# A Fourier mixing and SwiGLU kernel: earlier projection halves, an earlier rows load and later conversions in the head of the first batch

## Chip, cores and metric

The kernel runs on one core of a Trainium2 chip. The metric is the device time of one execution in microseconds (us); the time of a version is the median of several executions.

## The reference

Two blocks follow each other. The first mixes the 3008 positions of a sequence with a Fourier filter, for 8 sequences of 256 channels. The second is a SwiGLU network over the 8 x 3008 = 24064 rows that result.

```python
X = np.fft.rfft(x, axis=1)                       # x: (8, 3008, 256)
Y = X * (filt_r + 1j * filt_i)[None, :, :]       # filters: (1505, 256)
y = np.fft.irfft(Y, n=3008, axis=1)
g = y @ w_gate                                   # (24064, 256) @ (256, 1536)
silu = g * (1.0 / (1.0 + np.exp(-g)))
out = (silu * (y @ w_val)) @ w_out               # (1536, 256)
```

The three weight matrices arrive as 64-bit floats. The kernel itself has to turn them into 32-bit floats, from their bits.

## The kernel before

**Spectral part.** The transform of length 3008 = 47 x 64 is made of small dense transforms, each a matrix product on TensorE. For the first batch (`Spectral(0)`), stage 1 (`stage1_first`, then `turn`) transforms over 47 rows; stage 2a (L886) multiplies by a table, and VectorE (DVE) multiplies the result by the filter (L895, L899, L904), GpSimd (POOL) adds the two halves (L328); stage 2b (L921) multiplies by the table of the way back. There are 12 pieces u of stage 2 (`N_TWO`), and stage 2b runs four pieces behind stage 2a. ScalarE (ACT) copies each piece out of PSUM (L929) into a tile g. Each piece must then be regrouped before stage 3 (`stage3`, L970), which gives the tokens' values: pieces below `N_STORED` are stored to a tensor d2 in DRAM (`store_rest`) and read back into f0 by one load (`load_rows`), issued from POOL's queue; the later pieces go from g to f0 by small row copies on SP's queue (L934). Stores of the later pieces to d2 follow, since the chunks k = 1 to 3 of the batch are read from there (`load_t4`, L670, tile t). TensorE runs products on zeros (`idle`, L591) where it has nothing else to do.

**Network part.** The work is cut into chunks k of the sequence and groups g of hidden units (`Group`). One pair (k, g) is a step; a batch has 12. `SCHEDULE` is a list of 174 tokens that sets by hand the order of all instructions of a step on every engine; TensorE's hidden products are L1064, the output products L1161. Token t0.0 is the first product of the next chunk's stage 3 (tile pd). `combine_sequence` makes the sums of token values that some products need. Only in batch 0 are the steps ordered by g outside and k inside.

**Preparation of the weights.** `weight_halves` lists 36 halves of weights: for each of three groups 8 hidden halves ("hid") and 4 projection halves ("proj"). `load_weights(i)` loads half i (256 KB). `round_half(i)` rounds it, one step per call: DVE masks the mantissa (L405) and shifts the exponent (L408); ScalarE converts the mantissa (L410); the exponent is clamped either by DVE (L414, L417) or by ScalarE (L421, L423, L425); DVE puts in the sign (L428) and adds the low word (L432); POOL multiplies mantissa and exponent (L440, or L452 and L453) and makes sums. `combine_weights` makes further sums of hidden weights. The class `Preparation` gives each such step a tick: half i has a base tick, 4 after that of the half before (16 after half 7), and its steps follow at fixed distances. Ticks are executed at places written by hand: some between the pieces of stages 1 and 2, then at the places `tick_at` of each step of batch 0; `finish` executes what is due. So a tick is no time: it places instructions in the engines' program order. Buffers are few: raw words, `pw` (three) and w (two, and one in `wo_t` for every third half) are used again by later halves. `pin` fixes the order as written.

The order around the change: after stage 2a of piece 11, POOL loads halves 8 to 11 (L1255), then the rows; `finish(0)` runs the ticks up to 44; stage 2b of pieces 8 to 11 follows; SP issues the row copies, the stores of pieces 8 to 11 and the loads for chunk 1.

Of the kernel before, what the change touches and what calls it, by code (L numbers as in the profile page):

```python
# [43 lines left out]
AF = mybir.ActivationFunctionType  # L44
# [12 lines left out]
NK = 4 * NS  # L57
# [12 lines left out]
NV = 2  # L70
N_ONE = 32 // NV
N_TWO = NS // NV
N_QUAD = 8
N_FOUR = NS // 4
N_STORED = 8


WO = {1: 0, 7: 1, 2: 2, 3: 3, 5: 4, 6: 5, 4: 6}
# [25 lines left out]
BLOCKS = (0, 1, 3, 2)  # L104
# [101 lines left out]
def kernel(  # L206
# [10 lines left out]
    nc = tc.nc  # L217
# [157 lines left out]
        return spot if i < N_LENT and spot < 3 else None  # L375

    N_EARLY = 12

    def load_weights(i, queue=nc.sync):
        if i in raws or i >= len(weights):  # L380
# [9 lines left out]
    def round_half(i):  # L390


        raw, (use, *at) = raws[i], weights[i][1]
        low, high = raw[:, :, :, 0], raw[:, :, :, 1]
        pw = rpool.tile([128, 2, 128], U32, name=f"pw_{i}", tag="pw", bufs=3)
        if i % 3 == 2 and i < N_LENT:
            w = wo_t.rearrange("p j i f -> p (j i f)")[:, NJ * 7 * 128 - 256:]
            w = w.rearrange("p (b f) -> p b f", b=2)
        else:
            w = rpool.tile([128, 2, 128], FP32, name=f"w_{i}", tag="w", bufs=2)  # L400
        man = w.bitcast(U32)
        v = nc.vector
        flat = "p b f -> p (b f)"
        flat2 = "p b f two -> p (b f) two"
        pin(v.tensor_scalar(out=man, in0=high, scalar1=0xFFFFF, scalar2=None,  # L405
                            op0=ALU.bitwise_and))
        yield
        pin(v.tensor_scalar(out=pw, in0=high, scalar1=20, scalar2=0x7FF,  # L408
                            op0=ALU.logical_shift_right, op1=ALU.bitwise_and))
        pin(nc.scalar.activation(out=w, in_=man, func=AF.Copy, scale=2.0 ** -20, bias=1.0))  # L410
        yield
        pf = pw.bitcast(FP32)
        if i < 2 * len(BLOCKS):
            pin(v.tensor_scalar(out=pf, in0=pw, scalar1=-896.0, scalar2=0.0,  # L414
                                op0=ALU.add, op1=ALU.max))
            yield
            pin(v.tensor_scalar(out=pw, in0=pf, scalar1=255.0, scalar2=2.0 ** 23,  # L417
                                op0=ALU.min, op1=ALU.mult))
            yield
        else:  # L420
            pin(nc.scalar.activation(out=pf, in_=pw, func=AF.Relu, bias=off_t))  # L421
            yield
            pin(nc.scalar.activation(out=pf, in_=pf, func=AF.Relu, bias=top_t, scale=-1.0))  # L423
            yield
            pin(nc.scalar.activation(out=pw, in_=pf, func=AF.Copy, scale=-(2.0 ** 23),  # L425
                                     bias=255 * 2.0 ** 23))
            yield
        pin(v.scalar_tensor_tensor(out=pw.rearrange(flat), in0=raw.rearrange(flat2)[:, :, 1],  # L428
                                   scalar=0x80000000, in1=pw.rearrange(flat),
                                   op0=ALU.bitwise_and, op1=ALU.bitwise_or))  # L430
        yield
        pin(v.scalar_tensor_tensor(out=w.rearrange(flat), in0=raw.rearrange(flat2)[:, :, 0],  # L432
                                   scalar=2.0 ** -52, in1=w.rearrange(flat),
                                   op0=ALU.mult, op1=ALU.add))
        yield
        e = nc.gpsimd
        if use == "proj":
            j, l = at
            dst = wo_t[:, j]
            pin(e.tensor_tensor(out=dst[:, ts(l, 2), :], in0=w, in1=pf, op=ALU.mult))  # L440
            yield
            if l:
                b11, b12, b21, b22, t1, t2, t4 = [dst[:, i] for i in range(7)]
                pin(sub(e, t1, b12, b11))
                pin(sub(e, t2, b22, t1))
                pin(sub(e, b12, b22, b12))
                pin(sub(e, t4, b21, t2))
            return
        g, i, z = at
        wt = weights_of(0, 0, g)  # L450
        x, y, u = w[:, 0], wt[:, SLOT[f"Q{i}"], z], wt[:, SLOT[f"P{i}"], z]
        pin(e.tensor_tensor(out=y, in0=w[:, 1], in1=pf[:, 1], op=ALU.mult))  # L452
        pin(e.tensor_tensor(out=x if KS[i] else u, in0=x, in1=pf[:, 0], op=ALU.mult))  # L453
        yield
        if KS[i] == -1:
            pin(sub(e, u, x, y))
        elif KS[i]:
            pin(add(e, u, x, y))
            if KS[i] == 2:
                pin(add(e, u, u, y))  # L460
# [28 lines left out]
    class Preparation:  # L489
# [3 lines left out]
        def __init__(self):  # L493
            self.at, self.held = 0, []

            self.ticks, self.need = {}, {}
            base, ready = [], {}

            def put(t, f, by, pool=False):
                self.ticks.setdefault(t, ([], []))[pool].append(f)  # L500
                self.need[by] = max(self.need.get(by, 0), t)

            for i, (_, (use, *at)) in enumerate(weights):
                hid, g = use == "hid", at[0] if use == "hid" else at[0] // JB
                by = ((0, 3, 6) if hid else (1, 4, 7))[g]
                b = base[-1] + (4 if i != 2 * len(BLOCKS) else 16) if i else 0
                if i >= N_EARLY:
                    same = [n for n in range(N_EARLY, i) if spot_of(n) == spot_of(i)]
                    k = 2 if spot_of(i) is None else 1
                    last = base[same[-k]] + 8 if same[k - 1:] else 0  # L510
                    b = max(b, last + 8)
                    put(max(last, b - 10), lambda i=i: load_weights(i), by)
                base.append(b)
                if hid and g == NG - 1:
                    ready.setdefault(NT, b)
                half = []

                def go(half=half, i=i):
                    if not half:
                        half.append(round_half(i))  # L520
                    next(half[0], None)

                times = (0, 1, 2, 3, 4, 6, 7, 9, 10) if i >= 2 * len(BLOCKS) else \
                    (0, 1, 2, 3, 4, 6, 9, 10)
                for t in times:
                    put(b + t, go, by, t > 8 or t == 7)
                if hid and at[1:] == [BLOCKS[-1], 1]:
                    for n, pair in enumerate(PAIRS_USED):
                        c = combine_weights(g, *pair)
                        for t in range(3):  # L530

                            put(b + 11 + n + t, lambda c=c: next(c, None),
                                by if g or n < 4 else 1, t == 2)
            self.barriers = sorted((t, step) for step, t in ready.items())
            self.end = max(self.ticks)
# [22 lines left out]
        def finish(self, step):  # L558
            while any(s <= step and self.at <= t for s, t in self.need.items()):
# [1 line left out]
                self.tick(step)  # L561

    preparation = Preparation()
    tick_at = [set(range(40, 162, 6)), *[{n * 174 // 20 for n in range(20)}] * 2,
               {0, 6, 12, 18, 24, 31, 37, 42, 72, 78, 84, 90, 96, 102, 108, 114, 122, 130, 138, 146}]

    back_t, quad_t = [], []
# [26 lines left out]
    class Spectral:  # L594
# [345 lines left out]
            rows = self.d2_tokens.rearrange("n (p s) c -> (n p) (s c)", p=2)  # L940
            pin(queue.dma_start(out=rows[:, ts(u, NV * C)], in_=g.rearrange("q s c -> q (s c)")))

        def store_rest(self):

            for u, g in self.rest:
                self.load(out=self.d2_parts[:, ts(u, NV)], in_=g)
            self.rest = []

        def stage3(self, k, step):
# [241 lines left out]
    with tc.tile_pool(name="start", bufs=1) as spool0:  # L1191
# [12 lines left out]
        n = 0  # L1204
# [36 lines left out]
        for u in range(N_TWO + lag):  # L1241
            if u < N_TWO:
                spec.turn(u + 2)
                step = spec.stage2a(u)
                next(step)
                if u % 3 == 1:
                    spec.real_part(u + 2)
                next(step)
                preparation.tick(0, 2 * (u < 3), hold=True)
                run(step)  # L1250
                preparation.release()
                if u % 3 != 2:
                    spec.real_part(u + 1)
            if u == N_TWO:
                for i in range(8, N_EARLY):  # L1255
                    load_weights(i, nc.gpsimd)
                spec.load_rows(f0[0:8 * N_STORED, 0:2 * NH], 0, slice(0, 2 * N_STORED),
                               slice(0, 2 * NH), nc.gpsimd)
            if u == N_TWO + lag - 1:
                preparation.finish(0)  # L1260
            if u >= lag:
                if u == N_TWO:
                    idle(zero, [bank("idle")], 512)
                run(spec.stage2b(u - lag))
            if u == 6:
                pin(nc.sync.dma_start(out=wi_t, in_=wi_dram.ap()))
        for i in range(2):
            spec.t4[0, i] = f0[0:NK, ts(i, NH), :]
        spec.store_rest()
        for i in range(2):  # L1270
            spec.load_t4(1, i)

        idle(zero, [bank("idle") for _ in range(5)], 512)
        for step in (0, 2, 1, 3):
# [222 lines left out]
```

## Time and profile before

| | |
|---|---|
| median of 3 executions | 2826.43 us (2824.17 to 2828.59) |
| profiled execution | 2824.58 us |
| its span, first to last instruction | 2822.8 us |
| mean granted TensorE clock | 0.996 of full |
| TensorE busy | 2785.6 us (99%) |
| VectorE, ScalarE, GpSimd busy | 1994.4, 1565.0, 1573.9 us |
| data moved by DMA | 586.61 MB, mean 208 GB/s |

The profile comes from one execution, whose time is the span and what lies around it. PE is TensorE's matmuls, PEld its weight loads, SP the engine that only issues DMAs; SPq, ACTq and POOLq are issues of DMAs. In a timeline a row gives start and duration in us, engine, line, operation, the tile written and the tile read, and in brackets how long the engine stood idle before, and what ended that. A view of stages gives for each stretch the busy us of each engine with the number of instructions, the granted clock, the share of time that the DMA engines were busy and the GB/s moved. A matmul of 32-bit floats appears as two passes. Instructions of one engine run in program order, so one that waits holds up all behind it.

The first batch's spectral head takes the first 79 us; step 0 runs from there to about 108 us; steps 1 and later take about 29 us each.

### The profile page before, as it was taken

Reading aid. Unit: us, or ns where it says so; the run is one execution under the profiler, and the core shown is the slowest. Engines: PE = TensorE matmul, PEld = TensorE weight load, DVE = VectorE, ACT = ScalarE, POOL = GpSimd, SP = SyncE. Lnnn points to the kernel's source line nnn. Section 1 sums busy time; section 2 is a strip of 40 time slices with the busy share of each in tenths; the row PEclk is TensorE's granted clock in tenths of the full one; section 3 lists DMA queues with packets and bytes.
Section 4 is the critical chain, followed back from the end, with each engine's and each line's share of the span. In section 5 each row is a group of like instructions: output and inputs, shape, how many; then the busy total and the mean of one; then the engine's idle time right before and its main releaser. Section 6 shows DMA issues by size and latency. Waiting matters only on the chain.

```text
span 2822.8 us, 48516 instructions
## 1 busy us (share of the span) xinstructions
PE 2785.6 (99%) x15442; PEld 2319.7 (82%) x15442; DVE 1994.4 (71%) x4575; ACT 1565.0 (55%) x4182; POOL 1573.9 (56%) x1680
## 2 busy tenths in 40 slices
PE   8999999999999999999999999999999999999998
PEld 6777888888888888788888888878888888888886
DVE  7788776767666766667766677667676767666666
ACT  5776455655555555555555555555554555555553
POOL 4786575465545565456653566445655455545544
PEclk9999999999999999999999999999999999999999
DMA  8687876877666775667666676667766777654543
GB/s 224 201 276 244 272 243 212 288 234 238 181 188 203 248 224 172 204 216 229 221 184 198 210 250 198 189 189 239 225 207 178 215 224 229 190 155 145 153 136 82
DMA packets 363206, 586.61 MB, mean 208 GB/s; under 512 B 198348, under 2 KB 246476, under 8 KB 362792
## 3 DMA queue, kind: packets, MB, share of 16 engines
q1 hardware_dynamic: 338406, 534.17, 60.8%
q10 hardware_dynamic: 22354, 44.41, 5.8%
q0 software_dynamic: 2192, 4.91, 0.7%
q8 instruction: 126, 2.06, 0.3%
q14 instruction: 128, 1.05, 0.1%
HBM read 467.61 MB, written 101.34 MB: 202 GB/s over the span
## 4 chain that ended last, share of the span: by engine, by line
PE 91%; DVE 2%; POOL 1%; DMA 1%; ACT 0%; issue 0%; SPq 0%; POOLq 0%; ACTq 0%; DVEq 0%
PE wa L1064 25%; PE wk L1064 17%; PE wA L1161 17%; PE we L1064 12%; PE wG L1161 8%; PE wF L1161 4%; PE pd L967 3%; PE wqa L705 2%; PE wqc L764 1%; PE wqb L776 1%; DMA lent<-later_tbl 0%; PE pa L846 0%; POOL out_dram L1146 0%; POOL h L331 0%; PE pb L886 0%
## 5 line engine op out<-in xcount | busy, mean ns | idle before, releaser
L1064 PE MATMUL wa<-y_t,wt_t 128*128 128x188 f32 x4464 | 878.5, 323 | 3.9 <-ACT m L1099 2.7
L1064 PEld LDWEIGHTS wa<-y_t,wt_t 128*128 128x128 f32 x4464 | 746.8, 190 | 80.0 <-ACT wa L1090 8.9
L1064 PEld LDWEIGHTS wk<-y,wt_t 128*128 128x128 f32 x2976 | 495.4, 190 | 106.9 <-issue 33.4
L1064 PE MATMUL wk<-y,wt_t 128*128 128x188 f32 x2976 | 572.6, 325 | 0.8 <-ACT f L1079 0.8
L328 POOL TENSOR_TENSOR h<-h 128x376 f32<-128x376 f32 x190 | 183.5, 987 | 696.9 <-DVE h L1111 690.7
L331 POOL TENSOR_TENSOR h<-h 128x376 f32<-128x376 f32 x572 | 557.8, 997 | 15.4 <-DVE h L328 15.2
L1161 PE MATMUL wA<-h,wo_t 128*128 128x376 f32 x1532 | 550.9, 482 | 2.8 <-DVE o L328 2.1
L1064 PE MATMUL we<-y_t,wt_t 128*128 128x188 f32 x2232 | 431.8, 323 | 1.1 <-ACT we L1095 0.9
L331 POOL TENSOR_TENSOR D<-f,f 128x376 f32<-128x376 f32 x288 | 280.3, 987 | 257.3 <-ACT f L1079 253.6
L331 DVE TENSOR_TENSOR we<-we,m 128x376 f32<-128x376 f32 x576 | 319.9, 556 | 139.2 <-PE we L1064 71.3
L1064 PEld LDWEIGHTS we<-y_t,wt_t 128*128 128x128 f32 x2232 | 369.3, 190 | 2.3 <-ACT we L1095 1.7
L1161 PEld LDWEIGHTS wA<-h,wo_t 128*128 128x128 f32 x1532 | 275.3, 190 | 111.2 <-issue 7.2
L1099 ACT COPY m<-wa 128x376 f32<-128x376 f32 x576 | 272.6, 473 | 100.2 <-PE wa L1064 97.3
L335 DVE SCALAR_TENSOR_TENSOR y<-wk,c 128x376 f32<-128x376 f32 x480 | 244.5, 540 | 62.1 <-ACT c L1083 37.9
L1106 ACT ACTIVATE g<-wa 128x188 f32<-128x188 f32 x576 | 187.4, 326 | 165.3 <-PE wa L1064 155.9
L1106 ACT ACTIVATE u<-we 128x188 f32<-128x188 f32 x576 | 188.6, 327 | 160.4 <-DVE we L331 152.4
L1161 PE MATMUL wG<-h,wo_t 128*128 128x376 f32 x768 | 274.1, 479 | 0.0
L1083 ACT COPY c<-wk 128x376 f32<-128x376 f32 x288 | 136.5, 474 | 223.8 <-PE wk L1064 199.0
L1079 ACT ACTIVATE f<-wk 128x376 f32<-128x376 f32 x288 | 140.6, 488 | 169.3 <-PE wk L1064 118.1
L1095 ACT COPY we<-y 128x376 f32<-128x376 f32 x480 | 222.1, 479 | 17.8 <-DVE h L1111 11.8
L1111 DVE TENSOR_TENSOR h<-wa,g 128x188 f32<-128x188 f32 x576 | 198.9, 346 | 38.4 <-ACT g L1106 38.2
L1111 DVE TENSOR_TENSOR h<-we,u 128x188 f32<-128x188 f32 x576 | 198.1, 344 | 28.1 <-ACT u L1106 16.6
(165 smaller groups left out, 3519.0 us busy)
## 6 DMA issues: line engine op xcount, KB each, us to landing
wt_t<-w_all SPq DMA_DIRECT2D x174, 896.0 KB
wt_t<-w_all SPq DMA_DIRECT2D x174, 768.0 KB
lent<-filter SPq DMA_DIRECT2D x36, 1024.0 KB
lent<-d SPq DMA_DIRECT2D x84, 256.0 KB
d<-lent ACTq DMA_DIRECT2D x84, 256.0 KB
d<-lent ACTq DMA_DIRECT2D x96, 192.0 KB
lent<-raw SPq DMA_DIRECT2D x144, 128.0 KB
t<-d SPq DMA_DIRECT2D x112, 128.0 KB
```

The lines of the kernel that those rows point to most:

```text
L328: return eng.tensor_tensor(out=dst, in0=a, in1=b, op=ALU.add)
L331: return eng.tensor_tensor(out=dst, in0=a, in1=b, op=ALU.subtract)
L335: return nc.vector.scalar_tensor_tensor(out=dst, in0=a, scalar=-1.0, in1=b, op0=ALU.mult, op1=ALU.subtract)
L967: pin(nc.tensor.matmul(out=rows, lhsT=self.t4[k, i][:, j, ts(cb, 128)], rhs=cols, start=j == 0, stop=True, skip_group_check=True))
L1064: pin(nc.tensor.matmul(out=ps[:, z], lhsT=self.wt[:, SLOT[p], z], rhs=rhs, start=start and z == 0, stop=True, skip_group_check=True))
L1079: pin(act.mul(self.small(f"f{i}", f"f{i}", 1), t[f"k{i}"], -1.0))
L1083: pin(act.copy(out=self.small(f"c{i}", f"c{i}", 1), in_=t[f"k{i}"]))
L1095: pin(act.copy(out=self.bank(f"e{at}"), in_=t[f"y{at}"]))
L1099: pin(act.copy(out=self.small(f"m{at}", "m", 4), in_=t[f"a{at}"]))
L1106: pin(act.activation(out=self.small(op, "g", 3, 1)[:, 0], in_=ps[:, 1], func=AF.Silu))
L1111: pin(v.tensor_tensor(out=dst, in0=ps[:, 0], in1=g, op=ALU.mult))
L1161: pin(nc.tensor.matmul(out=self.tiles[at], lhsT=wo_t[:, JB * q + i, WO[p], :], rhs=self.hs[i][:, HID[p]], start=start and i == 0, stop=Tru ...
```

## The change

Nothing that is computed changes. (1) Piece 8 is now stored and read back with the pieces before it, so the rows load covers 72 rows of f0, not 64, and is issued one piece later. (2) Projection halves 8 to 11 are loaded from POOL's queue one at a time after pieces 5 to 8 of stage 2a, and no longer ahead of the rows load. (3) The stores of pieces 9 to 11 move from SP's queue to POOL's, behind a small copy on POOL that reads a column of f0 and so waits until f0 is complete. (4) Seven ticks of the preparation are executed ahead of stage 3, and in step 0 the ticks lie 7 tokens apart, not 6 (18 of them, not 21). (5) Half 8 takes the short way, with its exponent clamped by DVE. (6) ScalarE's conversion of the mantissa goes from tick 1 of a half to tick 3 (short way) or 4, its clamping from ticks 2 to 4 to ticks 3 to 5, and the rest of a long half by one tick, so that its last POOL step is at tick 11, not 10.

```diff
--- before.py
+++ after.py
@@ -72,7 +72,7 @@
 N_TWO = NS // NV
 N_QUAD = 8
 N_FOUR = NS // 4
-N_STORED = 8
+N_STORED = 9
 
 
 WO = {1: 0, 7: 1, 2: 2, 3: 3, 5: 4, 6: 5, 4: 6}
@@ -375,6 +375,7 @@
         return spot if i < N_LENT and spot < 3 else None
 
     N_EARLY = 12
+    N_SHORT = 9
 
     def load_weights(i, queue=nc.sync):
         if i in raws or i >= len(weights):
@@ -407,20 +408,21 @@
         yield
         pin(v.tensor_scalar(out=pw, in0=high, scalar1=20, scalar2=0x7FF,
                             op0=ALU.logical_shift_right, op1=ALU.bitwise_and))
-        pin(nc.scalar.activation(out=w, in_=man, func=AF.Copy, scale=2.0 ** -20, bias=1.0))
         yield
         pf = pw.bitcast(FP32)
-        if i < 2 * len(BLOCKS):
+        if i < N_SHORT:
             pin(v.tensor_scalar(out=pf, in0=pw, scalar1=-896.0, scalar2=0.0,
                                 op0=ALU.add, op1=ALU.max))
             yield
             pin(v.tensor_scalar(out=pw, in0=pf, scalar1=255.0, scalar2=2.0 ** 23,
                                 op0=ALU.min, op1=ALU.mult))
+            pin(nc.scalar.activation(out=w, in_=man, func=AF.Copy, scale=2.0 ** -20, bias=1.0))
             yield
         else:
             pin(nc.scalar.activation(out=pf, in_=pw, func=AF.Relu, bias=off_t))
             yield
             pin(nc.scalar.activation(out=pf, in_=pf, func=AF.Relu, bias=top_t, scale=-1.0))
+            pin(nc.scalar.activation(out=w, in_=man, func=AF.Copy, scale=2.0 ** -20, bias=1.0))
             yield
             pin(nc.scalar.activation(out=pw, in_=pf, func=AF.Copy, scale=-(2.0 ** 23),
                                      bias=255 * 2.0 ** 23))
@@ -507,7 +509,7 @@
                 if i >= N_EARLY:
                     same = [n for n in range(N_EARLY, i) if spot_of(n) == spot_of(i)]
                     k = 2 if spot_of(i) is None else 1
-                    last = base[same[-k]] + 8 if same[k - 1:] else 0
+                    last = base[same[-k]] + 9 if same[k - 1:] else 0
                     b = max(b, last + 8)
                     put(max(last, b - 10), lambda i=i: load_weights(i), by)
                 base.append(b)
@@ -520,10 +522,10 @@
                         half.append(round_half(i))
                     next(half[0], None)
 
-                times = (0, 1, 2, 3, 4, 6, 7, 9, 10) if i >= 2 * len(BLOCKS) else \
+                times = (0, 1, 3, 4, 5, 7, 8, 10, 11) if i >= N_SHORT else \
                     (0, 1, 2, 3, 4, 6, 9, 10)
                 for t in times:
-                    put(b + t, go, by, t > 8 or t == 7)
+                    put(b + t, go, by, t > 7)
                 if hid and at[1:] == [BLOCKS[-1], 1]:
                     for n, pair in enumerate(PAIRS_USED):
                         c = combine_weights(g, *pair)
@@ -561,7 +563,7 @@
                 self.tick(step)
 
     preparation = Preparation()
-    tick_at = [set(range(40, 162, 6)), *[{n * 174 // 20 for n in range(20)}] * 2,
+    tick_at = [set(range(40, 162, 7)), *[{n * 174 // 20 for n in range(20)}] * 2,
                {0, 6, 12, 18, 24, 31, 37, 42, 72, 78, 84, 90, 96, 102, 108, 114, 122, 130, 138, 146}]
 
     back_t, quad_t = [], []
@@ -940,10 +942,10 @@
             rows = self.d2_tokens.rearrange("n (p s) c -> (n p) (s c)", p=2)
             pin(queue.dma_start(out=rows[:, ts(u, NV * C)], in_=g.rearrange("q s c -> q (s c)")))
 
-        def store_rest(self):
+        def store_rest(self, queue=nc.sync):
 
             for u, g in self.rest:
-                self.load(out=self.d2_parts[:, ts(u, NV)], in_=g)
+                pin(queue.dma_start(out=self.d2_parts[:, ts(u, NV)], in_=g))
             self.rest = []
 
         def stage3(self, k, step):
@@ -1251,9 +1253,9 @@
                 preparation.release()
                 if u % 3 != 2:
                     spec.real_part(u + 1)
-            if u == N_TWO:
-                for i in range(8, N_EARLY):
-                    load_weights(i, nc.gpsimd)
+            if 5 <= u < 9:
+                load_weights(u + 3, nc.gpsimd)
+            if u == N_TWO + 1:
                 spec.load_rows(f0[0:8 * N_STORED, 0:2 * NH], 0, slice(0, 2 * N_STORED),
                                slice(0, 2 * NH), nc.gpsimd)
             if u == N_TWO + lag - 1:
@@ -1266,9 +1268,11 @@
                 pin(nc.sync.dma_start(out=wi_t, in_=wi_dram.ap()))
         for i in range(2):
             spec.t4[0, i] = f0[0:NK, ts(i, NH), :]
-        spec.store_rest()
+        pin(nc.gpsimd.tensor_copy(out=one[0:NK], in_=f0[0:NK, 0, 0:1]))
+        spec.store_rest(nc.gpsimd)
         for i in range(2):
             spec.load_t4(1, i)
+        preparation.tick(0, 7)
 
         idle(zero, [bank("idle") for _ in range(5)], 512)
         for step in (0, 2, 1, 3):
```

## The prediction

> **What bounds the kernel now.** I read first the busy times by stage, then TensorE's timeline at the head, then the queues that feed it, then the waits. By stage (columns: busy us, with instruction counts, of PE, PEld, DVE, ACT, POOL; then clock, DMA share, GB/s):
> ```profile
> 0.00:66.00 66.00, 59.56 (x306) 44.60 (x306) 51.32 (x107) 36.48 (x65) 33.17 (x52) 1.00 0.90 224
> 66.00:72.00 6.00, 0.10 (x1) 0.13 (x1) 0.00 (x0) 0.00 (x0) 0.00 (x0) 0.74 0.71 199
> 72.00:82.50 10.50, 10.50 (x47) 10.50 (x48) 2.17 (x5) 3.05 (x7) 1.94 (x2) 0.50 0.66 175
> 82.50:108.00 25.50, 21.44 (x128) 18.95 (x127) 23.31 (x58) 21.68 (x62) 17.75 (x25) 1.00 0.59 179
> 108.00:320.00 212.00, 203.71 (x1015) 164.28 (x1014) 183.28 (x391) 139.19 (x381) 153.65 (x196) 1.00 0.77 254
> 320.00:2822.00 2502.00, 2490.33 (x13952) 2081.20 (x13950) 1734.36 (x4016) 1364.61 (x3668) 1367.43 (x1407) 1.00 0.66 204
> ```
> After 320 us TensorE is 99.5% busy; the change touches only what is before. There TensorE idles 6 us at 66, runs 10.5 us at half clock, then waits 4 us in step 0, where DVE is busy 23.3 of 25.5. All that can be won: 6 + 5 + 4, and part of the 8 idle us between 108 and 320. TensorE's timeline shows the hole:
> ```profile
> 59.43 2.25 PE L921 MATMUL wpc<-room,tb 128*128 128x256 f32 x8 [0.51 <-POOL room L328]
> 61.52 4.46 PE L591 MATMUL widle<-room 128*128 128x512 f32 x10
> 71.90 7.11 PE L970 MATMUL wpd<-wi_t,f 96*128 96x94 f32 x32 [5.92 <-DMA f<-x]
> 78.80 1.52 PE L1064 MATMUL wk<-y,wt_t 128*128 128x188 f32 x4
> 80.11 1.86 PE L970 MATMUL pd<-wi_t,t 96*128 96x94 f32 x8
> ```
> Stage 3 waits for f0. Which load comes last? The waits name f<-x (SP's small rows), but the queues say otherwise:
> ```profile
> 58.11 1.27 POOL L328 TENSOR_TENSOR room<-room,y_t 128x512 f32<-128x512 f32 x1 [1.86 <-PE wpc L921]
> 60.65 2.39 POOL L388 DMA_DIRECT2D wo_t<-in_moe_w_out_dram  x4 [1.27 <-issue]
> 63.03 0.54 POOL L670 DMA_DIRECT2D f<-d  x1
> ```
> ```profile
> 58.85 5.46 SPq L934 DMA_DIRECT2D f<-x  x7
> 64.36 7.72 SPq L612 DMA_DIRECT2D d<-x  x4
> 74.49 1.71 SPq L670 DMA_DIRECT2D t<-d  x2
> ```
> The last SP row is issued by 64.3. The rows load f<-d stands behind 4 x 256 KB of weights and takes 8.0 us to land (view of DMA issues): 63.03 + 8.0 = 71.0, just ahead of 71.90. That is the load that ends the wait.
>
> **What the Trainium skill says.** (1) "TensorE: Matmul & The Clock Gate", Part 1: free-running windows of 3413 ns; an idle window halves the clock, a busy one restores it. Here the clock falls at 68.9 and returns at 82.5: 13.6 us, four windows, so agreed; but one busy window did not restore it (10.6 us of stage 3 at half clock did). At the tail a window with 1.2 us of matmuls in it still lost the clock (2816.6). (2) "DMA: Bandwidth & Descriptors", SWDGE vs HWDGE vs iDMA: the software queue of POOL and the queues of SP and ACT share 16 engines, which go round between them. Agrees: SP's four stores need 7.7 us while POOL's 1.5 MB is under way.
>
> **The change, part by part.** The profiled execution took 2824.58 us (span 2822.8), 1.85 below the median of 2826.43; I subtract from both.
>
> *Rows load first.* POOL is free at 59.38, so the load now waits for store 8 alone. Its copy ends, by ScalarE's timeline, 57.23 + 1.56 = 58.79; SP's issue 0.8; landing 2.4 (in the trace the last store's issue ends 72.08, the load that waits for it starts 74.49): 62.0. Then 576 KB: issue 0.5, and 3.3 (an estimate from the DMA page's "Anatomy of one DMA" section: 2.0 us + bytes at 436 GB/s) to 4.8 (the trace's median for the weight loads); I take 3.7 from the start of the issue: 65.7. SP loses two row issues (0.78 each) and gains one store, so its last row lands sooner than before.
>
> *Weights in the middle steps.* Four POOL issues of 0.6 us (2.39/4) between its adds: 2.4 us against idle 0.49 + 0.90 + 1.86 = 3.25 before its last add, so hidden; with the unexplained 1.27 on top of one, 0.4 us would show. The 1 MB is not free: DMA share is 0.88 to 0.96 until 52 and 0.4 from 54 to 58. One load (256 KB at 248 GB/s: 1.1 us) goes ahead of store 0, for which ScalarE already waits 2.5 us at 53.22. Queued behind that copy are the filter copies, for which DVE waits 0.63 at 55.48, and DVE has no other gap from 32.9 to 65. So it passes straight on: +1.1 us; bounds 0 (hidden) and 2.5 (two loads and a bit). f0 is whole at 66.8; the fillers (L591) end 65.98 + 1.1 = 67.1. Stage 3 starts 67.1: **4.8 earlier**, with no idle ahead of it, so at full clock.
>
> *Stage 3.* At full clock its steps are 0.87 apart (as L970's at 123.74 and 124.61): 3.5 us, not 6.9. With Q0's 0.65, TensorE asks for the next chunk's pd at 71.3, not 80.1.
>
> *Stores 9 to 11 behind the gate.* The copy to `one` holds them until f0 is whole. From 66.8: 0.15, three POOL issues 2.0, landing 2.4: SP's t<-d starts at 71.3 (before 74.49). How long that load took isn't shown; 393 KB at the 175 GB/s of that stretch is 2.2 us, and the engines took 1.5 us to begin (share 0.03 from 74 to 76), so 3.7: pd at 75.1. The floor is 2.9 by the DMA page's sum, the ceiling 5.6 (74.49 to 80.11). So TensorE idles 3.8 us **in a new place**; of the 8.8 us that it was ahead, **5.0 remain**. SP's weights, x and keeps are queued behind this wait; none is due for some 10 us.
>
> *Clock.* An idle 3.8 puts 2 us or more into some window; I expect a second drop of one to two windows, 5 us, costing 2.5. Before, 80.11 to 82.5 at half rate cost 1.2. **Loss 1.3** (0 drop: gain 1.2; three windows: loss 3.9).
>
> *Seven ticks ahead of stage 3, spacing 7.* Ticks 45 to 51 (two weight combinations, halves 8 and 9) move into the gap in which DVE is idle (65.6 to 77.4). Step 0 then runs 18 ticks, not 21 plus one at its end. From DVE's timeline, preparation took some 12.8 us of DVE's 23.3 there; 18 ticks with one operation each at about 0.55 are 9.9. DVE is relieved of 2.9, and ScalarE of four ticks, 1.8. Waits of TensorE there are 4 us; I take **2.5** (1 to 4). Half 8 goes over DVE wholly (two operations of 0.29 to 0.46 in place of three on ScalarE), in the gap: nothing.
>
> *Conversions two ticks behind.* ScalarE waited 9.6 us for L405 and 4.6 for L408 between 78 and 320; with L410 moved to tick 4 and L421 to 3 most of this goes, and what DVE and TensorE wait for ScalarE (TensorE: m 2.7, f 1.0, we 0.9) falls a little: 0.7. Against it, a half's last POOL operation is at tick 11, not 10, and its buffer w is rewritten by DVE at tick 12. DVE waited 2.7 us for POOL at L405 with two ticks' room; one is left. I charge 1.2. **Net loss 0.5** (gain 2 to loss 6).
>
> Sum: 5.0 - 1.3 + 2.5 - 0.5 = 5.7 us. 2824.58 - 5.7 = 2818.9 for a profiled execution, 2826.43 - 5.7 = **2820.7** for the median.
>
> **Rivals.** *A, the forecast*: gain 3 to 8, 2818.4 to 2823.4. *B, no second hole*: t lands nearly as TensorE asks (the load takes 2.9, stores land quickly) or no window catches the idle. For it: 8.8 us ahead at pd is more than A uses. Against: three transfers in series. Gain: A's 5.7, with 1.0 more at pd and 2.5 from the clock, 9.2: 2817.2. *C, the middle steps pay*: the weights delay stage 2 by 2.5, and t comes 5.6 after issue: 5.7 - 1.4 - 1.9 = 2.4: 2824.0. For it: DMA share 0.9 there. *D, slower*: DVE waits at L405 for POOL. POOL is 26.3 and 28.1 busy of 29 in the steps 108 to 137 and 137 to 166, so its order may lag by more than the one tick (28.9/20 = 1.45 us) that is left; 16 hidden halves at up to 1.45 are 23 us of DVE, which is 87% busy there; it decides once over 6 us reach TensorE on top of the charge. At 10 us: 2826.43 + 4.3 = 2830.7. Against: the waits with two ticks came only in 5 of 28 halves, the longest 1.3. That the change does nothing is excluded for the rows load, since in the new order no weight load stands between POOL's last add and it; that the gain is wholly hidden is C's end, 2826.4.
>
> **Chances.** A 0.50, B 0.20, C 0.20 (0 to 3 us gained), D 0.10. What a measurement tells from no change is about 0.2%, 5.7 us. Faster by more: B and a little over half of A, 0.46. Within: the rest of A, C, and D's 0.4 short of it, 0.48. Slower: 0.06. The range leaves out D and the outer half of B: 2816.8 to 2826.4.
>
> **What would show it.** Stage 3 (L970's first) starts near 67, at clock 1.00; POOL's rows load is issued near 62; ScalarE's wait for d<-x at 53 is 3.5; TensorE then waits some 4 us on t<-d and starts pd near 75; a half-clock stretch follows of 3 to 7 us; step 1 begins (wF, 108.19 before) near 102.5; TensorE's idle between there and 320 is near 8, DVE's waits at L405 for POOL under 5. I am wrong if stage 3 starts after 69, if pd starts before 73.5 or after 77, or if the idle after step 0 grows by more than 3.

## The result, and the profile after

The changed kernel takes 2833.36 us (2830.5 to 2837.3), the kernel before 2826.36 us on the same chip. The ratio is 1.0027, 95% interval [1.0016, 1.0038]: **7.0 us slower**, where 5.7 us faster was forecast. The profiled execution's span is 2830.9 us, the granted clock 0.995.

By stage, in the columns of the prediction, the changed kernel shows:

```profile
0.00:66.00 66.00, 59.23 (x306) 44.26 (x306) 52.17 (x110) 37.29 (x67) 33.16 (x52) 1.00 0.95 234
66.00:72.00 6.00, 0.56 (x3) 0.59 (x3) 2.38 (x9) 0.51 (x1) 0.25 (x2) 0.90 0.25 66
72.00:82.50 10.50, 7.86 (x35) 7.36 (x34) 2.17 (x5) 2.58 (x6) 4.51 (x6) 0.50 0.47 136
82.50:108.00 25.50, 22.89 (x128) 21.18 (x129) 18.77 (x48) 19.46 (x56) 16.73 (x22) 0.90 0.68 202
108.00:320.00 212.00, 199.71 (x980) 159.33 (x979) 175.79 (x376) 134.65 (x372) 151.37 (x197) 0.99 0.74 247
```

The hole from 66 to 72 is still there, and it is emptier: the DMA engines are 25% busy, not 71%. In the third row TensorE now idles 2.6 us that it did not idle before. In the last row it is busy 4.0 us less than before: it loses time long after the head. TensorE's timeline of the changed kernel:

```profile
60.87 4.46 PE L593 MATMUL widle<-room 128*128 128x512 f32 x10
71.44 7.11 PE L972 MATMUL wpd<-wi_t,f 96*128 96x94 f32 x32 [6.11 <-DMA f<-x]
78.34 1.52 PE L1066 MATMUL wk<-y,wt_t 128*128 128x188 f32 x4
82.93 2.02 PE L972 MATMUL pd<-wi_t,t 96*128 96x94 f32 x8 [3.07 <-DMA t<-d]
```

Stage 3 starts at 71.44, only 0.46 sooner than before, and again at half rate (7.11 us). Then pd waits for chunk 1's load, and comes at 82.93, 2.8 us later than before. The queues of the changed kernel say why. GpSimd's own, then SP's, then the rows load in the view of DMA issues (KB each, median us from issue to landing):

```profile
57.10 1.27 POOL L328 TENSOR_TENSOR room<-room,y_t 128x512 f32<-128x512 f32 x1 [0.49 <-DVE y_t L906]
62.40 0.61 POOL L672 DMA_DIRECT2D f<-d  x1 [4.03 <-ACT x L931]
71.46 0.18 POOL L1271 COPY one<-f 96x1 f32<-96x1 f32 x1 [8.45 <-DMA f<-x]
71.93 2.19 POOL L948 DMA_DIRECT2D d<-x  x3 [0.29 <-issue]
```
```profile
60.25 4.26 SPq L936 DMA_DIRECT2D f<-x  x5
77.78 1.69 SPq L672 DMA_DIRECT2D t<-d  x2
```
```profile
f<-d POOLq DMA_DIRECT2D x1, 576.0 KB, 7.3
```

The rows load is issued at 62.40, close to the forecast 62.0, but takes 7.3 us to land (69.71). The last row copies, issued by 63.8, land at 71.30, after it. Chunk 1's load is issued at 77.78, 6.3 us after f0 is whole, and pd starts 5.2 us after that.

Where the rest of the 7.0 us comes from is seen by comparing the start of the same product in both traces: the changed kernel is 0.65 us ahead at the end of stage 2 (61 us), 3.9 behind at 84, 1.45 behind where step 1 begins (109.65 against 108.19), 6.5 behind at 151, 9.3 at 163, 6.5 at 185 and 8.1 at 300 (times of the kernel before). So step 0 gives some 2.4 us back, and the steps after it lose 6.7.

### The profile page after: what moved, and what is told of

It is laid out like the page before. It is cut to its first block, busy times and chain, and to the rows that moved or that the text cites. A ratio compares the mean times of both kernels' runs of the same rounds, so it can differ in the third digit from the quotient of the medians.

```text
span 2830.9 us, 48533 instructions
## 1 busy us (share of the span) xinstructions
PE 2788.7 (99%) x15442; PEld 2321.3 (82%) x15442; DVE 1994.0 (70%) x4577; ACT 1563.8 (55%) x4179; POOL 1574.8 (56%) x1684
## 4 chain that ended last, share of the span: by engine, by line
PE 89%; POOL 1%; DVE 1%; DMA 1%; issue 0%; SPq 0%; ACT 0%; ACTq 0%; POOLq 0%; DVEq 0%
PE wa L1066 24%; PE wk L1066 16%; PE wA L1163 16%; PE we L1066 12%; PE wG L1163 8%; PE wF L1163 4%; PE pd L969 3%; PE wqa L707 2%; PE wqc L766 1%; PE wqb L778 1%; POOL h L331 0%; POOL out_dram L1148 0%; PE pc L923 0%; DMA lent<-later_tbl 0%; PE pb L888 0%
```

## Experiments

Theory after the result: (a) the head gained nothing because a load of 72 rows is slow and the gate then delays the stores; (b) the later ticks of the halves cost time in steps 1 to 5, as rival D had it. The rival to (a) is that POOL's queue or the moved weights are at fault; the rival to (b) that the late head or the half clock is carried on. Differences below are between the medians of a version and of the kernel before on the same chip; the intervals are about 2 us wide on each side, which is to be kept in mind for each single difference.

### The changed kernel with one part taken back

**64 rows** (e1), edit `N_STORED = 9` to `8`.

> The changed kernel with N_STORED back to 8: the rows load covers 64 rows, the row copies are 8 as before; all else stays. Theory (the load of 72 rows takes 7.3 us because it is spread over 9 DMA engines, as the landing events of its semaphore suggest, and holds up the row copies that share engines with it): the rows load is spread over 16 and lands within 5 us, f0 is complete near 68, stage 3 starts near 68 rather than 71.4, the execution is 2 to 5 us shorter than the changed kernel (2828 to 2831). Rival (the row copies on 4 engines are slow by themselves, and there are two more of them now): stage 3 starts at 71 or later, the time is 2833 or more.

Measured 2830.71 us, +4.4, ratio 1.0016 [1.001, 1.0023]. The rows load of this version:

```profile
f<-d POOLq DMA_DIRECT2D x1, 512.0 KB, 5.2
```

A ninth fewer bytes land in 5.2 us, not 7.3. A load's completion is counted in sixteen steps. In the trace of the 72 rows seven of them come together at 64.0, before the first packet of the load has ended (64.3), and the other nine from 67.7 to 69.7: nine engines carry it. With 64 rows all sixteen come from 64.7 to 65.5, with the data. The Trainium skill, "DMA: Bandwidth & Descriptors", "Why a DMA increments its semaphore by 16 and not by 1", says that the number of engines is the largest up to 16 that divides the outer sizes of both access patterns (what is read and what is written): 9 for 72 rows in 18 pieces, 16 for 64 rows in 16. It names an exception for some copies from GpSimd's queue, which these two loads are not: both traces agree with the rule. The last row copy now lands 5.0 us after its issue (62.84 to 67.83), not 7.5. Stage 3 begins at 68.03, but pd still waits 4.7 us for chunk 1's load, issued behind the gate at 73.94.

**No gate** (e2), the copy to `one` removed.

```diff
-        pin(nc.gpsimd.tensor_copy(out=one[0:NK], in_=f0[0:NK, 0, 0:1]))
```

> The changed kernel without the small copy on GpSimd that holds the stores of pieces 9 to 11 until f0 is complete; the stores stay on GpSimd's queue. Theory (the gate puts three transfers in series, and TensorE's new wait of 3.1 us for t is its price): t<-d is issued 3 to 5 us earlier, near 73 to 75, TensorE waits for t for less than 1 us, the time falls by 2 to 4 us to 2829 to 2831. Rival (without the gate the stores compete with the row copies for the engines, so stage 3 starts later by as much as is won): stage 3 starts at 73 or later and the time stays within 1.5 us of 2833.

Measured 2831.7 us, +5.4, ratio 1.0018 [1.0011, 1.0026]. That is 1.7 us less than the changed kernel, in the rival's range and not clear of noise. In its profiled execution, the slowest of all of this version, stage 2 was itself held up some 7 us by its stores, so its head's absolute times are no guide. Counted from the issue of the rows load, pd came 18.9 us later, in the changed kernel 20.5.

**The old times** (e3): the ticks of the halves and ScalarE's order as in the kernel before, all else as changed.

> The changed kernel with the ticks of a half as they were (ScalarE's mantissa conversion at tick 1, the last GpSimd step at tick 10); the head, the seven early ticks, the spacing of 7 and half 8 on the short way stay. Theory (the later ticks cost some 7 us in steps 1 and 2, since VectorE rewrites a buffer one tick after GpSimd's last use of it): the lag to the kernel before stays near 1.5 us from 108 to 320 instead of growing to 8, VectorE's waits for GpSimd at the mantissa line fall from 9.2 to some 3 us, the time is 2826 to 2828. Rival (the loss in steps 1 and 2 comes from the preparation running three ticks ahead of the steps): the lag still grows by 5 or more, the time is 2831 to 2834.

Measured 2829.6 us, +3.3, ratio 1.0012 [1.0006, 1.0019]. Its TensorE is 1.9 us behind from 112 to 148, 5.5 at 160, and about 3 from 185. Of the 7.0 us that the changed kernel loses between 112 and 300 this execution loses 1.6; by the medians 3.7 us are won. The time lies above what the theory expected, below the rival.

**64 rows and no gate** (e7), both edits together.

> The changed kernel with N_STORED back to 8 and without the gate copy. Theory (gate and 72 rows are separate costs): t<-d is issued before stage 3 ends and TensorE waits for t less than 1.5 us, against 4.7 with 64 rows and the gate; stage 3 starts by at most 2 us later than the 68.0 of that kernel; the time falls from 2830.7 to 2826.5 to 2829. Rival (without the gate the stores take the engines from the row copies, so that what is won at t is lost at f0): stage 3 starts at 71 or later and the time is 2830 or more.

Measured 2828.6 us, +2.0, ratio 1.001 [1.0003, 1.0016]. The chunk's load is issued at 69.77, and the second hole is gone:

```profile
70.12 7.11 PE L972 MATMUL wpd<-wi_t,f 96*128 96x94 f32 x32 [5.36 <-DMA f<-x]
78.33 1.86 PE L972 MATMUL pd<-wi_t,t 96*128 96x94 f32 x8
```

TensorE is 3.5 us ahead at 112, and yet 5.6 behind at 160 and 3.9 from 185: with a good head, about 7 us are lost after it in this execution. In it the clock was half from 114.1 to 121.0 and from 155.1 to 158.5, where the kernel before has full clock. By the medians the later ticks lose 3.0 of it (e9 below). Stage 3 begins 2.1 us later than with the gate (68.03): the stores now go beside the row copies, and that they delay them is likely but not shown.

### The kernel before with one part put in

**The later ticks alone** (e4), part 6 of the change in the kernel before.

```diff
-                    last = base[same[-k]] + 8 if same[k - 1:] else 0
+                    last = base[same[-k]] + 9 if same[k - 1:] else 0
...
-                times = (0, 1, 2, 3, 4, 6, 7, 9, 10) if i >= 2 * len(BLOCKS) else \
+                times = (0, 1, 3, 4, 5, 7, 8, 10, 11) if i >= 2 * len(BLOCKS) else \
...
-                    put(b + t, go, by, t > 8 or t == 7)
+                    put(b + t, go, by, t > 7)
```

> The kernel before with only the later ticks of a half (conversion at tick 3 or 4, last GpSimd step at 11). Theory (these ticks cost some 7 us in steps 1 and 2): the head is as before, TensorE falls behind by 5 to 8 us between 108 and 260, the time is 2831 to 2834. Rival (the loss comes from running ahead by three ticks, or from the head): the time is within 2 us of 2826.4.

Measured 2833.12 us, +6.8, ratio 1.0025 [1.0015, 1.0035]: as slow as the whole change. The head is as before (0.07 us behind at 112), then 3.35 behind at 124, 5.3 at 172, 6.2 at 300. So neither the head nor a half clock left over from it is the cause. One place shows rival D's wait. VectorE's mask in this version with the step behind it, GpSimd's steps ahead of the mask, and then the same two engines in the kernel before:

```profile
117.57 1.06 DVE L405 TENSOR_SCALAR w<-raw 128x256 uint32<-128x256 uint32 x1 [3.10 <-POOL lent L331]
118.55 1.20 DVE L433 SCALAR_TENSOR_TENSOR w<-wo_t,w 128x256 f32<-128x256 uint32 x1
```
```profile
116.12 1.00 POOL L331 TENSOR_TENSOR h<-h 128x376 f32<-128x376 f32 x1
117.07 0.47 POOL L331 TENSOR_TENSOR lent<-w,lent 128x128 f32<-128x128 f32 x1
```
```profile
115.41 1.13 DVE L432 SCALAR_TENSOR_TENSOR w<-wo_t,w 128x256 f32<-128x256 uint32 x1
116.46 0.53 DVE L328 TENSOR_TENSOR o<-o,wF 128x376 f32<-128x376 f32 x1
116.91 1.04 DVE L405 TENSOR_SCALAR w<-raw 128x256 uint32<-128x256 uint32 x1
```
```profile
115.26 0.99 POOL L331 TENSOR_TENSOR h<-h 128x376 f32<-128x376 f32 x1
116.21 0.64 POOL L331 TENSOR_TENSOR lent<-w,lent 128x128 f32<-128x128 f32 x1
```

The mask overwrites w, and must wait for the last step on GpSimd of the half that had w before. Before, the same mask waits for nothing. Behind the mask, VectorE's main work waits. GpSimd's step stands behind the same sum (h) in both; it is the mask that has moved. Since the projection halves now end one tick later, `finish` at the end of step 0 runs one tick more, and from there on every step that kept its tick comes one place earlier. The mask stands ahead of a sum of outputs (o) and of an older half's low word (L433), which it followed before (L432).

The waits at the mask sum to 5.0 us here from 108 to 262, and to 2.7 before, so 2.3 of the 6.8 us at most lie there. TensorE's own view of that stretch, before and here, shows where more of it lies:

```profile
108.00:262.00 154.00, 146.97 (x726) 115.58 (x725) 134.53 (x289) 109.43 (x303) 122.69 (x163) 1.00 0.77 253
```
```profile
108.00:262.00 154.00, 144.47 (x690) 113.66 (x690) 132.33 (x274) 105.17 (x292) 120.19 (x160) 0.97 0.74 245
```

TensorE idles only 2.5 us more, yet is 6.6 us behind at its end: it also ran slower. The clock was half from 123.4 to 126.8, from 167.8 to 171.2 and from 256.6 to 260.0, 10.2 us in all, and full throughout before. In the 3.4 us ahead of each of these TensorE was busy 1.5, 2.0 and 1.5 us. Over all executions the mean clock is 0.994 here and 0.996 before; 0.002 of 2830 us is at most some 5.7 us (an estimate).

**The same, with GpSimd's steps left at ticks 9 and 10** (e5), edit `times = (0, 1, 3, 4, 5, 7, 8, 9, 10)`.

> The kernel before with the later ticks for ScalarE and VectorE as in the changed kernel, but GpSimd's two steps of a half kept at ticks 9 and 10. Theory (the loss of the later ticks, 6.8 us when done alone, is VectorE waiting for GpSimd's last use of a buffer that it rewrites at tick 12): with the two ticks of room back the loss falls to under 2.5 us, 2825 to 2829, and VectorE's waits for GpSimd at the mantissa line from 5 us to under 3. Rival (the loss comes from ScalarE's work lying later, or from VectorE's own order, with the new mask ahead of the older half's last add): the time stays at 2831 to 2834.

Measured 2829.35 us, +2.7, ratio 1.0013 [1.0007, 1.002]. More than half of the loss goes, not all. But VectorE's waits at the mask hardly fall, from 5.0 us to 4.3, where under 3 was expected: what was won is not mainly these waits.

**GpSimd's steps later alone** (e6), edit `times = (0, 1, 2, 3, 4, 6, 7, 10, 11)`. As in e4, `finish` then runs one tick more: in the trace GpSimd's steps of the hidden halves keep their places among its sums, and VectorE's steps come earlier.

> The kernel before with nothing changed but GpSimd's two steps of a half, at ticks 10 and 11 and not 9 and 10. Theory (the room between GpSimd's last step and VectorE's next write is the cause): slower by 3 to 7 us, 2829.5 to 2833.5, with waits of VectorE for GpSimd at the mantissa line of 5 us or more. Rival (ScalarE's or VectorE's order is the cause): within 2 us of 2826.3.

Measured 2830.8 us, +4.2, ratio 1.0016 [1.0009, 1.0024]. Its profiled execution was already 4.1 us behind at 112, after a stage 2 held up by its stores, and lost only 1.3 to 2.5 after that: the medians say 4, this one trace less. The waits at the mask are 5.5 us, and the clock is full from 86 us to the tail.

**ScalarE's order alone** (e11), edit `times = (0, 1, 3, 4, 5, 6, 7, 9, 10)` with the mantissa's conversion moved as in the change.

> Before with ScalarE's conversions moved as in after (the mantissa one with the third exponent step, those steps at ticks 3, 4, 5 in place of 2, 3, 4), but VectorE's and POOL's steps of a half at the old ticks 6, 7, 9, 10. Theory (the later ticks lose by what they do to VectorE and POOL, not by ScalarE's order): 2826 to 2827.5 us. Rival (ScalarE's later conversions are themselves the loss): 2829 to 2833, with waits of VectorE on ScalarE's pw or w at ticks 6 and 7.

Measured 2826.16 us, +0.1, ratio 1.0 [0.9992, 1.0009]: no cost, and no gain either. Yet VectorE waits 5.3 us at the mask from 108 to 262, more than in e4, and TensorE falls only 0.7 us behind between 112 and 300. So the sum of these waits is no measure of what is lost.

**One tick more between the halves of a place** (e15), edit `+ 8` to `+ 9` alone.

> Before, with one tick more until the next half of a place is loaded and begun (9 in place of 8), every step of a half at its old tick. If the spacing is what is left of the later ticks' loss: 2828.5 to 2829.5 us. Rival (VectorE's steps one tick later are): 2826 to 2827.

Measured 2826.37 us, -0.5, ratio 1.0 [0.9992, 1.0009]. It is not the spacing.

**VectorE's two last steps later alone** (e17), edit `times = (0, 1, 2, 3, 4, 7, 8, 9, 10)`, with the spacing that it needs.

> Before, with VectorE's two last steps of a half at ticks 7 and 8 in place of 6 and 7 (and the load of the next half one tick later, as it must be), ScalarE and POOL at the old ticks. If VectorE's later steps are the rest of the loss: 2829 to 2830 us, PE about 3 us behind before at 281 us. Rival (ScalarE's and VectorE's delays cost only together): 2826 to 2827.5.

Measured 2831.04 us, +5.0, ratio 1.0019 [1.0011, 1.0026]. So VectorE's later steps cost time by themselves. But not through the mask: from 108 to 262 us, VectorE's waits at the mask are (us in total, times, longest):

```profile
DVE w L405 <- POOL lent L331: 1.5, 2, 1.2
DVE w L405 <- POOL lent L328: 1.3, 1, 1.3
DVE wo_t L405 <- POOL lent L328: 0.4, 1, 0.4
```

That is 3.2 us, against the 2.7 before. TensorE's waits in this stretch are 9.1 us, before 6.7, and they are spread over seven causes, none above 2.5. Two things differ in the trace. The older half's low word (L432) now stands behind the newer half's mask, where it stood ahead of it; and GpSimd, whose multiplication needs it one tick later, waits for it 12.4 us from 108 to 262, before 6.3. That this carries the 5.0 us is not shown. The clock is not the cause here: it is full from 86 us to the tail.

**Seven ticks and the spacing of 7 alone** (e8), with half 8's short way.

> The kernel before with the seven ticks ahead of stage 3, the spacing of 7 in step 0 and half 8 on the short way, nothing else. Theory (VectorE bounds step 0, and work moved into the gap at 66 to 77 us is won): stage 3 and the first pd start as before, step 1 starts 1.5 to 3.5 us earlier than 108.2, the time is 2822.5 to 2825.5. Rival (what step 0 gains is given back in steps 1 and 2, where GpSimd is as busy and now runs other work at these places): step 1 starts earlier but the time is within 1.5 us of 2826.3 or above.

Measured 2827.87 us, +1.3, ratio 1.0005 [0.9998, 1.0012]. Step 0 in its profile:

```profile
82.50:108.00 25.50, 21.88 (x126) 19.76 (x125) 20.43 (x51) 20.40 (x58) 19.66 (x27) 0.95 0.59 187
```

VectorE is relieved of 2.9 us (20.43 against 23.31), as forecast, but TensorE is busy only 0.4 more, and 0.1 us ahead at 112. At 160 it is 3.2 behind, and gets most of that back by 185.

### The head without the rest

**e9**: the changed kernel with 64 rows, no gate and the old times. **e10**: the kernel before with the moved weights, the rows load first and the stores in GpSimd's queue, nothing else. **e12**: the same with the stores left in SP's queue. The edit of e12:

```diff
-            if u == N_TWO:
-                for i in range(8, N_EARLY):
-                    load_weights(i, nc.gpsimd)
+            if 5 <= u < 9:
+                load_weights(u + 3, nc.gpsimd)
+            if u == N_TWO + 1:
```

> After with 64 stored rows, without the gate copy and with the old times: the seven ticks, the spacing of 7 and half 8's short way stay. Theory (the first step begins about 3.5 us sooner, as with 64 rows and no gate, and the old times give back the 7 us that the later ticks lose): 2823 to 2824.5 us, PE about 3 us ahead of before at 112 us and still 1 to 3 ahead at 300. Rival (a sooner first step only collides with the weight preparation, whatever the times are): 2826 to 2828, PE ahead at 112 and level by 200.

> Before with the projection halves loaded in the middle steps, the rows load first in its queue (64 rows) and the stores in POOL's queue; no gate, no extra ticks, old times. Theory: 2822 to 2823.5 us, about 1 less than with the seven ticks and the spacing of 7, which alone measured 1.3 over before. Rival (gain given back in the first step): 2825.5 to 2827.

> Before with part 1 alone: the four projection halves loaded in the middle steps and the rows load first in its queue; the stores stay in SP's queue. Theory (rows load lands about 5.2 us after its issue, stores follow the row copies on SP without a gate): stage 3 at 67 to 69 us against 71.9, total 2822.5 to 2825. Rival (stores on SP make the second hole as in before, and the gain of stage 3 goes to it): stage 3 sooner but pd no sooner than 80 us, total 2825.5 to 2827.

Measured 2825.05 (-1.0, ratio 0.9998 [0.999, 1.0007]), 2824.06 (-2.0, 0.9994 [0.9986, 1.0002]) and 2824.55 us (-1.5, 0.9994 [0.9986, 1.0003]). In none can the gain be told from nothing; e9 and e10 stay above what their theory expected. But all three keep the moved weights, and e9 and e10 the stores in GpSimd's queue, without a loss, which answers the rival to (a). In e12 stage 3 starts 2.3 us sooner than before, but at 112 only 1.2 is left. Stage 3 still runs at half rate:

```profile
69.64 7.11 PE L970 MATMUL wpd<-wi_t,f 96*128 96x94 f32 x32 [3.60 <-DMA f<-x]
77.85 1.86 PE L970 MATMUL pd<-wi_t,t 96*128 96x94 f32 x8
```

**Is it the clock?** e13 is e12 with 9 idle products ahead of stage 3, not 5; e14 is the kernel before with 11; e16 is e10 with 11.

```diff
-        idle(zero, [bank("idle") for _ in range(5)], 512)
+        idle(zero, [bank("idle") for _ in range(11)], 512)
```

> The version with the rows load first and the stores in SP's queue, and 9 idle matmuls ahead of stage 3 in place of 5, so that TensorE works through the wait. If the clock limits the head: stage 3's first 32 matmuls take 3.6 us in place of 7.1, PE is 4 to 5 us ahead of before at 112 us (1.2 without the filling), total 2820 to 2822. Rival (the values, the transposed rows and ScalarE's and VectorE's steps after them set the end of the head): stage 3 takes 3.6 us, then waits for its second operand until 77 us or so, PE is 1 to 2 us ahead at 112, total 2824 to 2825.5.

> Before, with 11 idle matmuls ahead of stage 3 in place of 5. If the clock limits the head: stage 3 takes 3.6 us, PE 3 us ahead at 112, total 2823. Rival (its second operand comes at 80 us whatever the clock): PE level with before at 112, within 1 us, total 2825.5 to 2827.

> The head alone (rows load first, stores in POOL's queue) with 11 idle matmuls ahead of stage 3 in place of 5. If the second operand's load sets the end of the head (issued at 70 to 71 us here, 73 with the stores in SP's queue): pd at 75 to 76 us, PE 3 to 4 us ahead at 112, total 2821.5 to 2823.5. Rival (the conversions that the first step needs, not the head's loads, are what comes next): PE no more than 1.6 us ahead at 112, total 2824 to 2825.

e13 measured 2824.91 us (-1.9, ratio 0.9993 [0.9985, 1.0001]), e14 2827.44 us (+0.6, 1.0001 [0.9993, 1.0009]; stage 3 in 5.7 us), e16 **2821.62 us (-4.4, 0.9984 [0.9978, 0.9991])**. TensorE's timeline of e13:

```profile
61.04 7.89 PE L591 MATMUL widle<-room 128*128 128x512 f32 x18
68.77 3.73 PE L970 MATMUL wpd<-wi_t,f 96*128 96x94 f32 x32
72.33 0.83 PE L1064 MATMUL wk<-y,wt_t 128*128 128x188 f32 x4
78.21 2.02 PE L970 MATMUL pd<-wi_t,t 96*128 96x94 f32 x8 [5.05 <-DMA t<-d]
```

and of e16:

```profile
59.78 9.61 PE L591 MATMUL widle<-room 128*128 128x512 f32 x22
69.52 3.78 PE L970 MATMUL wpd<-wi_t,f 96*128 96x94 f32 x32
73.14 0.83 PE L1064 MATMUL wk<-y,wt_t 128*128 128x188 f32 x4
74.63 1.13 PE L970 MATMUL pd<-wi_t,t 96*128 96x94 f32 x8 [0.66 <-DMA t<-d]
```

With the hole filled, stage 3 takes 3.7 to 3.8 us. In e13 the time that this saves becomes a wait of 5.05 us for chunk 1's load, which SP issues at 73.14, behind the row copies and stores. In e16 the stores are in GpSimd's queue without a gate, that load is issued at 69.17, and the wait is 0.66. TensorE is then 3.5 us ahead at 112, and is 3.5 ahead at 500. The two limits lie one behind the other: either change alone gains 2 us or less, both together 4.4. This version (e16) is faster than both kernels.

## Why the prediction was wrong, step by step

Five versions make a chain, each with one part more: e10 (the head) -2.0 us; with the seven ticks and the spacing of 7 (e9) -1.0; with the later ticks (e7) +2.0; with the gate (e1) +4.4; with the ninth piece (after) +7.0. The sum, 9.0 us, is clear of noise; a single step is known to some 3 us to either side only. For the gate and the ninth piece the traces say more: the wait of 4.7 us that comes with the gate, the landing of 7.3 us or 5.2.

- **Rows load first: failed in two places.** *"SP loses two row issues (0.78 each) and gains one store, so its last row lands sooner than before"* and *"That is the load that ends the wait"* set the profile's own answer aside. The wait was put down to f<-x, and that was right: in the kernel before the rows load landed at 71.01, SP's last row copy at 71.70, and stage 3 began at 71.90. A row copy of 32 KB, issued at 63.7, needed 8.0 us there. In the changed kernel it needed 7.5 to 8.1. The prediction took the end of an issue for the end of a transfer. That SP's four stores "need 7.7 us" was a sign of it: 5.8 of the 7.7 SP stood waiting for a row copy to land. The last row copy did land sooner than before, but by 0.4 us (71.30), not with the forecast f0 at 66.8. The term "3.7 from the start of the issue" was 7.3: it took the bytes from 64 rows to 72, and not the engines from 16 to 9; even on sixteen it measured 5.2 (e1). The ninth piece costs 2.6 us by the medians.
- **Weights in the middle steps: charged too much.** Charged 1.1, bounds 0 and 2.5; in the traces no cost is to be seen. TensorE was 0.65 us ahead at the end of stage 2, and ScalarE's wait for its stores near 53 was 2.6 us, before 2.5, where 3.5 was forecast.
- **Stage 3 at full clock: failed**, since the hole stayed: 7.11 us, not 3.5. e13 and e14 show that the clock is worth little while chunk 1's load comes late.
- **Stores behind the gate: right in kind, too small.** From f0 whole to the load's issue 4.5 was forecast, 6.3 measured; from there to pd 3.7 and 5.2. "5.0 remain" became -2.8 at pd. The floor of 2.9 for this load rests on the sum that the Trainium skill, "DMA: Bandwidth & Descriptors", "Anatomy of one DMA", gives for GpSimd's queue, and the load is SP's; it took 5.1. The gate costs 1.6 us (e2) to 2.4 (e1 against e7) by the medians, neither clear of noise.
- **Clock: too small.** Forecast was a second drop of one or two windows. The records show half clock from 70.7 to 87.8, in one piece, and once more from 258.5 to 261.9, against 68.9 to 82.5 before. What it cost between pd and 84 us, 1.1 us (2.8 to 3.9 behind), is near the 1.3 charged, but by luck: there was no second drop there, the first went on.
- **Seven ticks, spacing 7: the term of 2.5 failed.** Alone it measured +1.3 us (by the interval -0.6 to +3.4). The relief of VectorE by 2.9 us was right, but TensorE went on waiting: for ScalarE's m 4.3 us from 78 to 262 (before 2.7), for GpSimd's sum y_t 1.8 (before 0.8). Busy time saved on an engine was priced as time of the path.
- **Conversions two ticks behind: "Net loss 0.5" failed, and rival D came instead.** The parts: ScalarE's order, forecast to gain 0.7, measured +0.1. VectorE's and GpSimd's later steps, charged 1.2, cost 6.8 alone, 3.0 (e9 to e7) to 3.7 (e3) beside the other parts. The waits of the changed kernel from 108 to 262 us, VectorE's first, then TensorE's from 78 to 640:

```profile
DVE w L406 <- POOL lent L331: 3.5, 1, 3.5
DVE w L406 <- POOL lent L328: 3.4, 3, 1.8
DVE wo_t L406 <- POOL lent L328: 2.1, 1, 2.1
DVE wa L1088 <- POOL D L331: 2.3, 1, 2.3
```
```profile
PE wa L1066 <- DVE wa L1088: 7.6, 7, 2.8
PE pd L972 <- DMA t<-d: 3.1, 1, 3.1
```

VectorE waits at the mask 9.2 us in all, where "under 5" was forecast, in a few long waits and not in many short ones; D had priced 16 halves at up to 1.45. And TensorE waits for VectorE's wa 7.6 us, before 2.3. That the later ticks cost this is shown (e3, e4), and that GpSimd's steps have a part in it (e5). D's wait is seen in its place (e4), but that it carries the loss is not shown: the waits at the mask sum to 5.3 us in e11, which loses nothing, to 4.3 in e5 (+2.7), 5.0 in e4 (+6.8) and 3.2 in e17 (+5.0). A second carrier, which neither the forecast nor D had, is the clock in the steps: over all executions its mean is 0.994 in e4 and in the changed kernel, 0.996 before. In e6 and e17 the clock is as before, and what carries their loss stays open. So does why e17 with ScalarE's order added (e5) costs less than e17 (their intervals overlap), and why the later ticks cost less beside the other parts than alone.

In sum, three terms failed. The gain of 5.0 in the head was lost because the row copies and the load on nine engines, not the place of the rows load in its queue, set when f0 was whole, and because the gate put chunk 1's load behind them. The gain of 2.5 from step 0 was not there. The loss of 0.5 from the conversions was 3.0 to 6.8. D was given 0.10 because the waits with two ticks' room were few and short; how they and TensorE's own waits grow when a tick is taken was not in that trace.

## What to carry to other kernels

When a view names the transfer that ends a wait, check when each candidate landed, not when it was issued, before another is put in its place. A tick or slot that lies between the last reader of a buffer and its next writer is not idle; and moving one step can move where all others stand, as `finish` did here, so write out the new order of each engine before a price is put on it. Do not take a sum of waits on a helper engine for the loss: compare it with a version that waits as long and loses nothing (e11), and look at the clock in the same stretch. Where two transfers and a clock limit the same stretch one behind the other, each change alone shows little; try them together before one is dropped.

## What was not expected of the hardware

- A load of 72 rows (576 KB) landed in 7.3 us on nine engines, one of 64 rows (512 KB) in 5.2 on sixteen.
- Row copies of 32 KB needed 7.5 to 8.1 us beside it, 5.0 beside the load of 64 rows (the last one); while only they were left (69.7 to 71.3), the DMA engines were busy 0.09.
- A hole of 3.6 us ahead of stage 3 (e12) brought half clock just as one of 6 did: from 68.4 to 82.0. With idle products in the hole (e16) the clock stayed full until 83.1, where it fell for 10.2 us after waits of 2.1 us and less.
- In e4 each of three waits of 1.3 to 1.9 us in TensorE's steps was followed by 3.4 us at half clock.
